# Attention and a linear-attention layer side by side: a build-time scheduler in place of a fixed slot order, seven pooled PSUM banks, unpadded projections, short first and last units

## Chip, cores and metric

The kernel runs on one core of one Trainium2 chip. The metric is the device time of one execution in microseconds, taken without the profiler; the median of three runs counts. The profile is of another execution, with the profiler on.

## What is computed

Two independent layers on 2048 tokens of width 512, with 32 heads of 16 features each, written side by side into one output of 2048 x 1024.

```python
def _A_ref(x, wqkv, wo):          # softmax attention
    qkv = (x @ wqkv).reshape(B, S, 3, H, Dh).transpose(2, 0, 3, 1, 4)
    q, k, v = qkv[0], qkv[1], qkv[2]
    scores = jnp.einsum("bhqd,bhkd->bhqk", q, k) * Dh ** -0.5
    p = softmax(scores, axis=-1)
    o = jnp.einsum("bhqk,bhkd->bhqd", p, v)
    return o.transpose(0, 2, 1, 3).reshape(B, S, D) @ wo

def _B_ref(x, wqkv, w_phi, wo):   # linear attention
    ...
    pq = jnp.einsum("bhsd,hdf->bhsf", q, w_phi)
    pk = jnp.einsum("bhsd,hdf->bhsf", k, w_phi)
    phi_q = concatenate([softmax(pq), softmax(-pq)])
    phi_k = concatenate([softmax(pk), softmax(-pk)])
    kv = jnp.einsum("bhsf,bhsd->bhfd", phi_k, v)
    z  = jnp.einsum("bhsf->bhf", phi_k)
    num = jnp.einsum("bhqf,bhfd->bhqd", phi_q, kv)
    den = jnp.einsum("bhqf,bhf->bhq", phi_q, z)[..., None] + 1e-6
    return (num / den).transpose(0, 2, 1, 3).reshape(B, S, D) @ wo
```

All inputs are bf16. Nearly all of the work is in layer A: 32 heads x 2048 queries x 2048 keys of scores and exponentials.

## The kernel before

**Units and passes.** The 32 heads are taken in 8 groups of 4 (the letter g), the queries in 4 chunks of 512 (c). A unit is one group and one chunk: 32 units, ordered by chunk, then by group (line 118). Each head of a group has 32 rows of `QT` and `KT`: 16 for its features, the others for helper rows. `WQp` and `WKp` are the projection weights padded to that layout, so that one projection job (`proj`, line 318) gives the Q or K of one group and 512 tokens.

A unit has its scores computed twice. The first time (**M1**, `emit_m1`, line 715) a matmul gives 128 queries x 512 keys of a head; two heads at once fill two of PSUM's banks 0 to 3, and VectorE takes the maximum over the keys of both with one reduce of 128x1024 (`emit_r1`, line 730). 32 such pairs make a unit. Then the **maxima chain** (`emit_mchain`, line 739) runs: a row maximum on VectorE, three short GpSimd instructions that split the negated maximum into a high and a low bf16 part, a transposing DMA, and two DMAs that put both parts into helper rows of `QT`. The second time (**M2**, `emit_m2`, line 766) the matmul gives 128 keys x 512 queries with the maximum already subtracted through the helper rows, and ScalarE writes the exponential to `pT`, a ring of 16 tiles (`emit_exp`, line 779). **PV** (`emit_pv`, line 787) multiplies by V with a column of ones, four heads side by side, into bank 7. At a unit's end `emit_xev` copies bank 7 out, the sums go through two small DMAs, a logarithm and an exponential (`emit_ln`, `emit_ex`), are spread by four DMAs (line 849), and GpSimd multiplies (`emit_mul`).

**Slots.** The order is written out by hand, in the loop over `tau` at line 916. Slot `tau` holds M1 pair `tau`, the M2 pair of slot `tau - LAG`, two exponentials, perhaps a PV of 4 matmuls, perhaps a piece of a background job, fills, and the reduce of this slot's pair. `LAG` is 43: the 32 slots of a unit and `LAGX` = 11 for the maxima chain. There are 1024 M1 slots, and 46 more until the last PV (`PVLAG` = 3). M1 waits for the reduce of two slots before. M2 takes a bank from `ring_free`, which holds banks 4, 5 and 6; a background job (`bg_step`, line 280) takes one of the same three and runs one piece a slot, as a rule four matmuls of 128x512.

**Jobs** are the projections of A, the output projections, and all matmuls of layer B (`fold_job`, `fm`, `v_job`, `kv_job`, `y_job`, `ob_job`). `fm` is a chain for 128 tokens of Q or K: projection, copy, two reduces of 128x512 on VectorE (lines 462 and 464), GpSimd and ScalarE steps, spaced over later slots by hand. A new one starts every 26 slots from slot 172.

**Fills** (`emit_fill`, line 813) are matmuls on zeros that add nothing: a slot that has fewer than two groups of PV or job work gets groups of four until it has two.

**Queues.** Every engine carries out its instructions in the order in which the plan appended them; a wait stops whatever is behind it. All transfers but a few at both ends go through SP's queue, in that order too.

**The end.** The last unit's PV comes with a second set of matmuls that give the sums spread over partitions (line 804); `emit_last` (line 879) normalises and finishes the last four output tiles.

Of the kernel before, what the change touches and what calls it, by code (L numbers as in the profile page):

```python
# [1 line left out]

# [4 lines left out]
ALU = mybir.AluOpType  # L7
# [86 lines left out]

def bass_concat_heads__softmax_full_mha__linear_kernel_hedgehog__prompt_kernel(
# [8 lines left out]
    NKT = S // 128  # L104
    NKC = S // 512
    NQC = S // 512
    NQ = 8 * NKC
    NB = 4 * NKT
    NU = NG * NQC
    RING = 16  # L110
    LAGX = 11
    PVLAG = 3
    RMLAG = 1
    NCOL = 2
    LAG = NQ + LAGX
    FM0 = 172
    FMSTEP = 26
    units = [(g, c) for c in range(NQC) for g in range(NG)]

    with contextlib.ExitStack() as es:  # L120
# [8 lines left out]
        P.add_stream("sp", None)  # L129

        def dsem(name):
            P.add_stream(name, es.enter_context(nc.semaphore("d_" + name)), 16)
            return name

        def last_tok(key):
            s = P.streams[key]
            clock = dict(s.known)
            clock[key] = s.seq
            return _Tok(key, s.seq, clock)

        PS = es.enter_context(nc.psum_tensor("PS", [128, 8, 512], F32))
        bank_reader = {}

        ones_t = sb("ones_t", [128, 128], BF)
        ident = sb("ident", [128, 128], BF)
        zmv = sb("zmv", [128, 512], BF)
        bias_k = sb("bias_k", [128, 1], F32)
        eps_t = sb("eps_t", [128, 1], F32)
# [5 lines left out]
        WQp = sb("WQp", [128, 4, NG, 128], BF)  # L154
        WKp = sb("WKp", [128, 4, NG, 128], BF)
# [9 lines left out]
        part = sb("part", [128, 2, 4, 4, NKC], F32)  # L165
        mrow = sb("mrow", [128, 2, 16], F32)
        trow = sb("trow", [128, 2, 16], F32)
        BD = sb("BD", [128, 4, 128], BF)
        woB = sb("woB", [128, 4, 512], BF)
        qmask = sb("qmask", [128, 4], F32)  # L170
        pB = sb("pB", [128, 2, 512], F32)
        uB = sb("uB", [128, 2, 1024], F32)
# [4 lines left out]
        vB = sb("vB", [128, 4, 544], BF)  # L177

        def flat(t):
# [3 lines left out]
        wqf = flat(WQp)  # L183
        wkf = flat(WKp)
# [3 lines left out]
        Wf = wkf.rearrange("p (x t c) -> p x t c", x=2, t=4)  # L188
        phiT = wqf[:, 0:2048].rearrange("p (a t s) -> p a t s", a=2, t=8)
        yB = wqf[:, 2048:3136].bitcast(F32)  # L190
        oB = wqf[:, 3136:3648]
# [6 lines left out]
        t_ones = P.op("pool", lambda e: e.memset(ones_t[:], 1.0))  # L198
        t_ident = P.op("pool", lambda e: e.affine_select(
            ident[:], ones_t[:], pattern=[[1, 128]], base=0, channel_multiplier=-1,  # L200
            compare_op=ALU.is_equal, fill=0.0), [t_ones])
        t_zmv = P.op("pool", lambda e: e.memset(zmv[:].bitcast(U32), 0))

        t_wa = {}
        wa_v = A_wqkv.rearrange("(ct p) n -> p ct n", p=128)

        def load_w(queue, i):
            t_wa[i] = P.dma(queue, dsem("wa%d" % i), lambda e: e.dma_start(
                wA[:, :, i * 512:(i + 1) * 512], wa_v[:, :, i * 512:(i + 1) * 512]))

        load_w("act", 0)
        load_w("act", 1)
        t_xa = {}
        for c in range(NQC):
            d = dsem("xa%d" % c)
            if c == 1:
                load_w("sp", 2)
            for ct in range(4):
                t_xa[c] = P.dma("sp", d, lambda e, ct=ct, c=c: e.dma_start_transpose(
                    xAT[:, ct, c * 512:(c + 1) * 512], A_x[0][c * 512:(c + 1) * 512, ct * 128:(ct + 1) * 128]))  # L220

        t_wq0 = P.op("dve", lambda e: e.memset(wqf.bitcast(U32), 0))
        t_wk0 = P.op("dve", lambda e: e.memset(wkf.bitcast(U32), 0))
        t_bias = P.op("dve", lambda e: e.tensor_reduce(
            bias_k[:, :], ident[:].rearrange("p (r x) -> p r x", x=32)[:, :, 16:18], AX.XY, ALU.add), [t_ident])

        def pad_copy(dst, col0, dep0):
            src = wA[:, :, col0:col0 + 512].rearrange("p ct (gr d) -> p ct gr d", d=16)
            dv = dst[:].rearrange("p ct g (r x) -> p ct (g r) x", x=32)[:, :, :, 0:16]
            return P.op("dve", lambda e: e.tensor_copy(dv, src), [t_wa[col0 // 512], dep0])  # L230

        t_wqp = pad_copy(WQp, 0, t_wq0)
        t_wkp = pad_copy(WKp, 512, t_wk0)

        t_stage0 = P.op("pool", lambda e: e.memset(flat(stage).bitcast(U32), 0), [t_wkp])
        t_bd0 = P.op("pool", lambda e: e.memset(flat(BD).bitcast(U32), 0))
        t_wo0 = P.op("pool", lambda e: e.memset(flat(WOp).bitcast(U32), 0))
        t_vp1 = P.op("pool", lambda e: e.memset(VP[:, :, :, 16:17], 1.0))
        t_yd1 = P.op("pool", lambda e: e.memset(Yd[:], 1.0))
        t_vb1 = P.op("pool", lambda e: e.memset(vB[:], 1.0))  # L240
        t_eps = P.op("pool", lambda e: e.memset(eps_t[:], 1e-6))
        t_qm = P.op("pool", lambda e: e.memset(qmask[:], 1.0))
        t_qm = P.op("pool", lambda e: e.affine_select(
# [9 lines left out]
        for r in range(4):  # L253
            t_wo = P.dma("sp", d_wo, lambda e, r=r: e.dma_start(
                WOp[32 * r:32 * r + 16, :, :], wo_v[r]), [t_wo0])

        calls = {}
        jobs = []  # L260
        running = []
# [741 lines left out]
```

## Time and profile before

| | us |
|---|---|
| median of three timed runs | 1343.72 |
| lowest and highest of them | 1342.71, 1344.74 |
| span of the profiled execution | 3156.6 |

The profiled execution took 2.35 times as long as the timed ones. What lies around a span (launch and end) isn't recorded. In the page, busy time is given for each engine, with its share of the span; a group of instructions has its line, its engine, output and inputs with shapes, the count, then busy time, mean ns of one, and the idle time before them with what ended it. In a timeline a row has the start, the length, engine, line and operation; rows with x2 or more are merged neighbours.

| stretch of the profiled execution, us | PE busy | DVE busy | ACT busy | granted clock |
|---|---|---|---|---|
| 0 to 30 | 28.33 | 4.84 | 1.28 | 1.00 |
| 70 to 150 | 80.00 | 16.81 | 6.43 | 1.00 |
| 300 to 600 | 300.00 | 96.61 | 97.58 | 1.00 |
| 1000 to 2000 | 999.36 | 479.75 | 461.41 | 1.00 |
| 3000 to 3156 | 155.30 | 10.07 | 57.23 | 1.00 |

The first reduce starts at 43.4 us and the last at 3013.9; the first exponential starts at 302.7 and the last at 3138.7.

### The profile page before, as it was taken

What the parts mean: (1) busy time and instruction counts of PE and PEld (TensorE: products, weight loads), DVE (VectorE), ACT (ScalarE), POOL (GpSimd) and SP (SyncE); (2) the same over time, 40 slices, a digit from 0 to 9 for tenths busy, and PEclk for the clock granted to TensorE, in tenths of its full rate; (3) what the DMA queues carried; (4) which work ended last, traced back from release to release, by engine and by line L of the source; (5) the groups of instructions that cost most, each with busy time, mean ns of one, the idle gap of its engine ahead of it and who ended that gap; (6) DMA issues with size and microseconds to landing.
All of it is one profiled execution on the core that took longest, in us unless ns stands there. A gap on an engine that the chain in (4) does not pass through costs nothing.

```text
span 3156.6 us, 29062 instructions
## 1 busy us (share of the span) xinstructions
PE 3152.2 (100%) x12226; PEld 362.2 (11%) x12226; DVE 1304.1 (41%) x1130; ACT 1296.2 (41%) x2479; POOL 307.0 (10%) x423
## 2 busy tenths in 40 slices
PE   9999999999999999999999999999999999999999
PEld 1111001111111111110011111111111111111111
DVE  1222223444444544544454435444454444445410
ACT  0001223444444444444444435444444444444442
POOL 1000000000011111111111101111111111111100
DMA  2000001000000000000000000000000000100000
GB/s 53 0 0 24 0 11 18 8 2 3 2 2 3 3 6 6 3 3 3 3 3 3 3 8 7 11 11 10 13 10 11 10 16 11 13 10 10 11 5 7
DMA packets 68939, 26.66 MB, mean 8 GB/s; under 512 B 59656, under 2 KB 66824, under 8 KB 68808
## 3 DMA queue, kind: packets, MB, share of 16 engines
q1 hardware_dynamic: 67464, 23.49, 5.4%
q8 instruction: 96, 1.57, 0.2%
q10 hardware_dynamic: 1344, 1.31, 0.1%
q14 instruction: 35, 0.29, 0.0%
HBM read 3.16 MB, written 4.19 MB: 2 GB/s over the span
## 4 chain that ended last, share of the span: by engine, by line
PE 99%; issue 0%; ACT 0%; POOL 0%; DVE 0%; POOLq 0%
PE PS L823 35%; PE PS L723 28%; PE PS L796 11%; PE PS L333 8%; PE PS L452 3%; PE PS L321 3%; PE PS L661 3%; PE PS L528 2%; PE PS L634 2%; PE PS L771 2%; PE PS L369 1%; PE PS L874 1%; PE PS L804 1%; PE PS L589 0%; PE PS L541 0%
## 5 line engine op out<-in xcount | busy, mean ns | idle before, releaser
L735 DVE TENSOR_REDUCE part<-PS 128x2 f32<-128x1024 f32 x1024 | 1255.2, 1226 | 1676.9 <-PE PS L723 1007.5
L782 ACT ACTIVATE pT<-PS 128x512 bf16<-128x512 f32 x2048 | 1111.5, 594 | 1262.1 <-PE PS L771 663.9
L823 PE MATMUL PS<-zmv,ones_t 128*17 128x512 bf16 x5004 | 1217.8, 973 | 0.3 <-ACT pT L782 0.3
L723 PE MATMUL PS<-KT,QT 32*128 32x512 bf16 x2048 | 959.5, 931 | 0.8 <-DVE QT L341 0.8
L771 PE MATMUL PS<-QT,KT 32*128 32x512 bf16 x2048 | 932.2, 902 | 0.0
L796 PE MATMUL PS<-pT,VP 128*17 128x512 bf16 x2048 | 457.2, 782 | 0.0
L723 PEld LDWEIGHTS PS<-KT,QT 32*128 32x128 bf16 x2048 | 111.0, 101 | 1580.8 <-DVE part L735 1102.9
L333 PE MATMUL PS<-xAT,WKp 128*128 128x512 bf16 x128 | 151.8, 1446 | 0.0
L823 PEld LDWEIGHTS PS<-zmv,ones_t 128*17 128x17 bf16 x5004 | 88.9, 88 | 315.1 <-issue 298.6
L771 PEld LDWEIGHTS PS<-QT,KT 32*128 32x128 bf16 x2048 | 111.1, 101 | 64.9 <-ACT pT L782 51.5
L333 PE MATMUL PS<-xAT,WQp 128*128 128x512 bf16 x128 | 116.5, 1122 | 0.0
L748 POOL TENSOR_SCALAR stage<-mrow 128x16 bf16<-128x16 f32 x32 | 8.1, 253 | 1070.4 <-DVE mrow L744 1070.4
L452 PE MATMUL PS<-WKp,xBT 128*128 128x512 bf16 x128 | 106.8, 1051 | 0.0
L345 ACT ACTIVATE KT<-PS,bias_k 128x512 bf16<-128x512 f32 x32 | 22.0, 687 | 194.9 <-PE PS L333 194.9
L507 POOL TENSOR_TENSOR wA<-eB,rB 128x1024 bf16<-128x1024 bf16 x32 | 61.7, 1929 | 398.1 <-ACT rB L501 398.1
L796 PEld LDWEIGHTS PS<-pT,VP 128*17 128x17 bf16 x2048 | 49.6, 87 | 378.0 <-issue 356.3
L321 PE MATMUL PS<-wA,xAT 128*128 128x512 bf16 x64 | 84.3, 1598 | 0.0
L859 POOL TENSOR_TENSOR QT<-X,Yd 128x256 bf16<-128x256 f32 x62 | 43.6, 725 | 400.6 <-DMA Yd<-Yd 400.4
L661 PE MATMUL PS<-WOp,QT 128*128 128x512 bf16 x96 | 80.8, 1063 | 0.0
L486 POOL TENSOR_TENSOR sB<-eB 128x512 f32<-128x512 bf16 x32 | 36.9, 1154 | 374.5 <-ACT eB L479 374.5
L471 POOL TENSOR_TENSOR uB<-pB,mB 128x512 f32<-128x512 f32 x32 | 33.9, 1058 | 395.9 <-DVE mB L462 395.9
L309 ACT ACTIVATE QT<-PS 128x512 bf16<-128x512 f32 x31 | 18.5, 597 | 93.7 <-PE PS L333 93.7
(78 smaller groups left out, 713.8 us busy)
## 6 DMA issues: line engine op xcount, KB each, us to landing
Yd<-Yd SPq DMA_DIRECT2D x124, 32.0 KB, 3.2
out_dram<-xAT SPq DMA_DIRECT2D x16, 128.0 KB, 1.7
out_dram<-OA SPq DMA_DIRECT2D x12, 128.0 KB, 1.7
wA<-in_A_wqkv_dram ACTq DMA_DIRECT2D x2, 512.0 KB, 5.0
QT<-mcols SPq DMA_DIRECT2D x64, 4.0 KB
wA<-in_A_wqkv_dram SPq DMA_DIRECT2D x1, 512.0 KB, 4.3
WOp<-in_A_wo_dram SPq DMA_DIRECT2D x4, 128.0 KB, 4.4
BD<-in_B_w_phi_dram SPq DMA_DIRECT2D x32, 0.5 KB, 1.6
```

What stands on the lines that cost most here:

```text
L321: piece = mm_piece(4, lambda e, b, ct: e.matmul(PS[:, b, :], xAT[:, ct, kt * 128:(kt + 1) * 128], wA[:, ct, 1024:1536], start=(ct == 0), s ...
L333: piece = mm_piece(4, lambda e, b, ct: e.matmul(PS[:, b, :], wpad[:, ct, g, :], xAT[:, ct, c * 512:(c + 1) * 512], start=(ct == 0), stop=( ...
L452: add_job(slot, [mm_piece(4, lambda e, b, ct: e.matmul(PS[:, b, :], xBT[:, ct, st * 128:(st + 1) * 128], Wf[:, x, ct, :], start=(ct == 0), ...
L528: piece = mm_piece(4, lambda e, b, ct: e.matmul(PS[:, b, :], xBT[:, ct, st * 128:(st + 1) * 128], wA[:, ct, 0:512], start=(ct == 0), stop= ...
L634: piece = mm_piece(4, lambda e, b, t: e.matmul(PS[:, b, :], oTB[:, i, t, :], woB[:, t, :], start=(t == 0), stop=(t == 3)), lambda: [cx["ot ...
L661: return mm_piece(4, lambda e, b, i: e.matmul(PS[:, b, :], QT[:, 4 * p + i, st * 128:(st + 1) * 128], WOp[:, 4 * p + i, :], start=(p == 0 ...
L723: tok = P.op("pe", lambda e, r=r: e.matmul(PS[:, r, :], QT[32 * r:32 * r + 32, g, q0:q0 + 128], KT[32 * r:32 * r + 32, g, kc * 512:(kc + 1 ...
L735: r1[q1] = P.op("dve", lambda e: e.tensor_reduce(part[:, u % 2, 2 * half:2 * half + 2, qt, kc], PS[:, 2 * half:2 * half + 2, :], AX.X, ALU ...
L771: m2_t[B] = P.op("pe", lambda e: e.matmul(PS[:, bank, :], KT[32 * r:32 * r + 32, g, kt * 128:(kt + 1) * 128], QT[32 * r:32 * r + 32, g, c ...
L782: exp_t[B] = P.op("act", lambda e: e.activation(pT[:, slot, :], PS[:, bank, :], ACT.Exp, scale=0.25), [m2_t[B], slot_reader.get(slot)])
L796: tok = P.op("pe", lambda e, B=B, r=r: e.matmul(PVB[32 * r:32 * r + 17, :], VP[:, kt, 4 * g + r, :], pT[:, B % RING, :], start=(kt == 0), ...
L823: P.op("pe", lambda e, cq=cq: e.matmul(PS[32 * cq:32 * cq + 17, bank, :], ones_t[:, 0:17], zmv[:, :], start=(bank != 7), stop=(bank != 7), ...
```

## The change

The loop over slots, its fixed lags and the hand-written spacing go. In their place the program, while it is being built, plays an event-driven model: every instruction is a node with an engine, what it waits for, how long it is taken to occupy its engine and when its result is taken to be there. At each event the model looks at each free engine and picks what it starts next; the order of picking becomes the order of the queues. The built kernel is still static; semaphores still guard every wait.

- **PSUM.** Bank 7 stays PV's. Banks 0 to 6 are one pool: an M1 pair wants two neighbours (or one bank at a time, then each with its own reduce of 128x512), an M2 tile one, a job one. At most 4 banks are held by M1, 3 by M2 (2 when a job is at hand), 1 by jobs.
- **TensorE's order** (`try_pe`): M1 or M2 first, by which of VectorE and ScalarE has less work waiting, then PV, the last output tile's matmuls, jobs (in pieces of two matmuls, if that doesn't delay M1), then fills, only while the array was less than 46% active over the last 3.4 us by the model's count. M2 of a unit is placed as soon as the model has its maxima landed.
- **Projections.** `WQp` and `WKp` go, with their memsets and padded copies. One job now gives eight heads (two groups) for 512 tokens, with weights straight from `wA`. Heads of even and odd number interleave in the 32-row blocks; a mask by row keeps one group's 16 rows and puts 0 or 1 in the others. For the first four groups the mask is applied as ScalarE (for the first Q, VectorE) copies out of PSUM, twice a job; for the others ScalarE copies once to `SG` and GpSimd masks twice.
- **Units.** The first and the last unit are cut into four of 128 queries: 38 units. In a short unit an M2 tile holds four key tiles x 128 queries, so that an exponential is still 128x512. The maxima of the first four may be found interleaved, as key chunks arrive.
- **Smaller ones.** The 32 loads of `w_phi` become one and four masked copies on GpSimd; the output weights of A come in eight transfers for four; layer B's scratch no longer lies in the projection weights; one `uB` buffer for two; `fm` chains are released every 31.5 us of model time from 45 us on; the end finishes one output tile for four.

```diff
-    LAG = NQ + LAGX
-    units = [(g, c) for c in range(NQC) for g in range(NG)]
+            cuts = [(0, 512)]
+            if (g, c) in ((0, 0), (NG - 1, NC - 1)):
+                cuts = [(128 * i, 128) for i in range(4)]
+            for q0, nq in cuts:
+                units.append((g, c, 512 * c + q0, nq))
...
-        t_wqp = pad_copy(WQp, 0, t_wq0)
-        t_wkp = pad_copy(WKp, 512, t_wk0)
...
-        ring_free = [4, 5, 6]
+        bank_free = {b: 0.0 for b in range(7)}
...
+        def act(out_, in_, func, cols, reads=(), writes=(), deps=(), prio=5, sbuf=False, at=0.0, **kw):
+            c = cols / 1200.0
+            return mk("act", lambda ds: P.op("act", lambda e: e.activation(out_(), in_(), func, **kw), ds),
+                      reads, writes, deps, occ=c + (0.093 if sbuf else 0.067) + (0.093 if "bias" in kw else 0.0),
+                      lat=c + (0.28 if sbuf else 0.26) + (0.093 if "bias" in kw else 0.0), prio=prio, at=at)
+
+        def dve(fn, cols, reads=(), writes=(), deps=(), prio=5, at=0.0):
+            c = cols / 960.0
+            return mk("dve", lambda ds: P.op("dve", fn, ds), reads, writes, deps, occ=c + 0.07, lat=c + 0.24,
+                      prio=prio, at=at)
...
+            j = job(quads(lambda e, b, ct: e.matmul(
+                PS[:, b, :], wA[:, ct, col:col + 128], xAT[:, ct, sl], start=(ct == 0), stop=(ct == 3))),
...
+            evac(j, act(lambda: SG[:, k, :], lambda: PS[:, j.bank, :], ACT.Copy, 512, (), [("SG", k)], prio=2))
+            for gl in range(2):
+                g = 2 * G + gl
+                if kind == "q":
+                    kq_nodes[(kind, g, c)] = pool(lambda e, g=g, gl=gl: e.tensor_scalar(
+                        T[:, g, sl], SG[:, k, :], kmask[:, gl:gl + 1], None, ALU.mult), 0.7,
+                        [("SG", k), "kmask"], [(K, g, c)], prio=1)
...
+            nf = nfree()
+            if held["m"] >= 4 or nf < 1:
+                return False
+            k = 2
+            half = sm["half"]
+            if half is not None or not pair_free() or held["m"] > 2:
+                if not single and half is None:
+                    return False
+                k = 1
...
+            dma("mt%d" % ub, lambda e: e.dma_start_transpose(mcols[:, ub, :], stage[:, ub, :]), [("stage", ub)],
+                [("mcols", ub)], prio=0, us=1.15, land=2.4)
...
+        def try_m2():
...
+            if not all(done_by(n, now) for n in mr_nodes[u]):
+                return False
+            if nfree() < 1 or held["e"] >= (EMAX - 1 if held["g"] or job_ready(now) else EMAX):
+                return False
...
+        def try_fill():
+            now = state["now"]
+            while area and area[0][0] < now - 3.4:
+                area.pop(0)
+            if "end" in state or not vz[0]:
+                return False
+            low = now < 9.0 or sum(a for _, a in area) < FILL * 3.4
...
+        def try_pe():
...
+            d, a = backlog("dve"), backlog("act")
+            TM = 3
+            TA = 3
+            for e in (("dve", "act") if d <= a else ("act", "dve")):
+                if e == "dve" and d < TM and try_m1(d < 0.3):
+                    return True
+                if e == "act" and a < TA and slots_ready() and try_m2():
+                    return True
...
+            if hurts(0.213 if pv_width() == 512 else 0.06) <= 0.03 or pv_urgent():
+                if try_pv():
+                    return True
+            if try_acc():
+                return True
+            if hurts(0.43) <= JL + job_late(now) and try_job():
+                return True
+            return hurts(0.22) <= 0.03 and try_fill()
...
-        while tau <= max(pv_in_slot) or jobs or running or calls:
-            if tau < total_q1:
-                emit_m1(tau)
...
+        while True:
+            if not events:
+                break
+            t = heapq.heappop(events)
...
+                for k in ENGS:
+                    if free[k] <= state["now"] + 1e-6:
...
+                        if try_pe() if k == "pe" else try_eng(k):
+                            go = True
```

## The prediction, made before the changed kernel was run

> **What bounds the kernel now.** I began with the page's first and fourth parts, busy times and the chain that ended last, because the profiled span is 2.3 times the median of the timed runs (1343.72 us) and that has to be understood first.
>
> ```profile
> span 3156.6 us, 29062 instructions
> PE 3152.2 (100%) x12226; PEld 362.2 (11%) x12226; DVE 1304.1 (41%) x1130; ACT 1296.2 (41%) x2479; POOL 307.0 (10%) x423
> ...
> PE 99%; issue 0%; ACT 0%; POOL 0%; DVE 0%; POOLq 0%
> ```
>
> In this execution TensorE is never idle and is the whole chain. It can't have been so in the timed runs: PE's 3152 us of work fitted into 1344. The timeline of one slot shows why.
>
> ```profile
> 908.62 1.75 PE L823 MATMUL PS<-zmv,ones_t 128*17 128x512 bf16 x8
> 908.73 1.23 DVE L735 TENSOR_REDUCE part<-PS 128x2 f32<-128x1024 f32 x1 [3.65 <-PE PS L771]
> ...
> 909.87 0.67 DVE L462 TENSOR_REDUCE mB<-pB 128x32 f32<-128x512 f32 x1
> ...
> 910.46 0.68 DVE L464 TENSOR_REDUCE mB<-pB 128x32 f32<-128x512 f32 x1
> ...
> 911.28 1.09 ACT L782 ACTIVATE pT<-PS 128x512 bf16<-128x512 f32 x2 [1.44 <-PE PS L723]
> ```
>
> Eight fills are two passes (four run side by side in the array), and later passes start about 0.84 us apart. I count passes of 512 columns from the page and the list of groups: fills 5004/4 = 1251; scores of both kinds 1067 (line 723's pair and line 771's pair run side by side); PV 512, its sums 16; full-width matmuls 726; small ones about 42. Together 3614 passes; at 0.84 us 3036 us, the rest being a slower first 300 us. Timed, a pass can have taken at most 1343.7/3614 = 0.372 us. The granted clock reads 1.00 throughout, so the record doesn't show the slowdown. [...]
>
> VectorE and ScalarE durations don't hang on that clock, so they carry the sum. The rows show what two instructions cost back to back, which is less than their durations: the reduce of 1024 starts at 908.73, the next at 909.87, so **1.14 us** (duration 1.23); the reduce of 512 costs 0.59; two exponentials together take 1.085, so a second one adds **0.49 us** (0.594 alone). Then the groups by cost:
>
> ```profile
> L735 DVE TENSOR_REDUCE part<-PS 128x2 f32<-128x1024 f32 x1024 | 1255.2, 1226 | 1676.9 <-PE PS L723 1007.5
> L782 ACT ACTIVATE pT<-PS 128x512 bf16<-128x512 f32 x2048 | 1111.5, 594 | 1262.1 <-PE PS L771 663.9
> L823 PE MATMUL PS<-zmv,ones_t 128*17 128x512 bf16 x5004 | 1217.8, 973 | 0.3 <-ACT pT L782 0.3
> ```
>
> VectorE at full pace: 1024 x 1.14 = 1167, feature-map reduces 64 x 0.59 = 38, row maxima 32 x 0.21 = 7: 1212 us, 1.18 a slot. ScalarE: 2048 x 0.49 = 1006; its other 431 instructions are 184.7 us, less some 0.10 overlap each, 142: 1148 us, 1.12 a slot. VectorE is the bound, ScalarE 5% behind.
>
> The median, split by this: about 13 us before the first reduce (the first transposed loads are issued by 5.9 us and land 2.8 later, then eight projection matmuls, one 0.69 us copy, the first scores). At the end no maxima are left for 43 slots (LAG) and three more until the last PV: 46 x 0.98 = 45 us at two exponentials a slot, then about 7 for logarithm, exponential, product, matmul, copy and output. So 1344 - 13 - 52 = 1279 us for 1024 slots, 1.249 each: VectorE idles 1279 - 1212 = **67 us** inside the slots. These three terms (13, 52, 67) are estimates; the median fixes only their sum, 132.
>
> **The change, part by part.**
>
> *Last unit in four pieces of 128 queries.* The 52 us tail becomes: the row-maximum chain of one piece, then a quarter of the exponentials. The chain now:
>
> ```profile
> 900.78 0.21 DVE L744 TENSOR_REDUCE mrow<-part 128x16 f32<-128x64 f32 x1
> ...
> 901.08 0.25 POOL L748 TENSOR_SCALAR stage<-mrow 128x16 bf16<-128x16 f32 x1 [21.38 <-DVE mrow L744]
> 901.41 0.22 POOL L750 TENSOR_TENSOR trow<-mrow,stage 128x16 f32<-128x16 f32 x1
> 901.72 0.25 POOL L751 TENSOR_SCALAR stage<-trow 128x16 bf16<-128x16 f32 x1
> 902.00 1.12 SPq L753 DMA_TRANSPOSE mcols<-stage  x1
> ...
> 904.27 1.20 SPq L756 DMA_DIRECT2D QT<-mcols  x2
> ```
>
> From 900.78 to the second DMA's issue at about 904.9; no row shows its landing. Nearest are 1.7 (output) and 3.2 us (Yd<-Yd); I take 2.0, so 6.1 + 0.1 of queueing, about 6. Then 16 exponentials x 0.49 = 8, PV and closing steps 7: **21 us**, range 20 to 23. Gain 31.
>
> *First unit in four pieces.* ScalarE's first exponential, now after 43 slots (13 + 43 x 1.249 = 67 us), comes once a 128-query piece has met all four key chunks. The last chunk's transposed loads are issued until 22.1 us and land 2.8 later, so about 26 + 6 = 33 us. But VectorE is the bound, so these 34 us only free ScalarE; I take nothing for it. Cover: VectorE's lead of 66 us over ScalarE; were that gone, the 34 us would count.
>
> The six extra units cost VectorE 6 x 0.21, ScalarE 6 x (a 128-wide copy of about 0.2, two short steps of 0.14) = 3 us, SP 6 x 8 DMA issues of 0.6 to 1.1 = some 35 us of queue, beside the other work.
>
> *Eight-head projections.* Q and K jobs drop from 64 to 32: 128 full matmuls, 128 passes off TensorE. ScalarE's copies drop from 63 to 40 (16 direct K, 2 direct Q, 22 staged): 23 x 0.49 + 16 biases x 0.09 = 13 us off. GpSimd gains 44 maskings of 128x512; the list has none. Nearest by size: 128x256 f32 at 0.725 and 128x512 at 1.06; so 32 to 47 us, I take 40. GpSimd goes from 307 to about 347 of some 1260 us: off the path unless a masking (about 1 us) stands before line 748's successors, 38 x 1 us at worst; taken at nothing, because only the order of Pool's own queue decides and the chain is put first in it. The memsets and padded copies at the head (1.76 x 2, 0.68 x 2 on VectorE) go; the first transposed load lands no earlier, and Q's first copies become two: head gain 0, range -2 to +2.
>
> *The planned order.* VectorE must still do 1024 x 1.14 + 38 + 38 x 0.21 + 1.4 = **1214 us**. A score pair may be split in two single banks: 2 x 0.59 - 1.14 = 0.04 us more each, 0 to 41 us if all were; I take 100, 4 us. What is left is the 67 us of idleness. Now M1's pair stands on PE's queue behind the M2 pair, which needs one of three banks, of which a job holds one; and a slot with a job and PV has six passes, up to 2.2 us against 1.14. There are some 240 job pieces; 67/240 = 0.28 us each. After, 32 pieces are gone, the rest come in halves of two matmuls and only when a bank is free and VectorE has work in hand. Bounds: 0 (the plan holds exactly) and 67 (it gains nothing). I take 0.08 us for each of 208, **16 us**, nearer the lower end because fills leave too: TensorE's passes fall from 3614 to about 2200 plus fills, at most 0.372 x 2200 = 818 us of 1260.
>
> Sum: 13 + 1214 + 4 + 16 + 21 = **1268 us**, 76 less than 1344 (31 tail, 51 idleness, 6 dearer on VectorE).
>
> **Rivals.**
>
> *A. Idleness stays at 67 us.* It would if it comes from signal latencies between PE and VectorE. For it: line 723's weight load waits 1102.9 us for VectorE in the list of waits, so the two hand over every slot. Against: that is a slow-pass execution. 1252 + 67 = 1319.
>
> *B. The plan holds exactly*: 1248. For it: 1.14 and 0.49 repeat to 0.01. Against: DMA landings scatter (transpose of the maxima 2.2 to 4.1 us).
>
> *C. Slower: M2 at the head of TensorE's queue.* The next unit's M2 waits for its maxima. Today LAGX gives the chain 11 slots, 13.7 us for about 6. The new order issues M2 when the chain is planned to end, without that slack; behind the waiting M2 stand M1 and PV, so VectorE starves once its two filled pairs (2.3 us) are used. 38 units x (lateness - 2.3): slower than before from (1346.4 - 1268)/38 = 2.1, a lateness of 4.4 us a unit. The transpose's worst is 1.8 over its median, which speaks against; SP's queue, where chain DMAs can stand behind a transfer waiting for ScalarE (782.5 us of such waits at line 834), speaks for. At 5.5 us late: 1268 + 38 x 3.2 = 1390.
>
> *D. TensorE becomes the bound.* With 2200 passes, a pass longer than 1214/2200 = 0.55 us would do it; at 0.60 it gives 1320 + 34 = 1354. In the trace the granted clock never falls, but the fills never stop either. [...]
>
> **How the numbers follow.** Forecast 0.58, A 0.20, B 0.08, C 0.09, D 0.05. C is all slower; of D I give 0.02 to slower, 0.01 to same, 0.02 to faster. So faster 0.88, same 0.01, slower 0.11, with 0.2% (2.7 us) as what a measurement of this kernel tells from none. The range holds forecast, A and B: from B less 4 us of pitch error, 1244, to A plus 5, 1324; it leaves out C and most of D, 0.14.
>
> **What would show it.** Right: if the profile is again of the slow kind, its span falls to passes x 0.84, (2200 + some 500 fills) x 0.84 = about 2270 us; if not, VectorE is busy 95% or more between its first and last reduce, starts the last 20 to 23 us before the end, and most of its idle time is short. A shows as short gaps before nearly every reduce; C as long gaps of VectorE and ScalarE together once a unit, ended by the maxima's DMA; D as a chain of waits on TensorE with a granted clock of 0.5. Wrong also if Pool's maskings end waits of the maxima chain, or if pairs are split far more than 100 times.

## The result, and the profile after

The changed kernel is **slower**: 1684.63 us, median of 4 runs (1672.45 to 1725.32), against 1344.23 (1342.71 to 1345.11) for the kernel before on the same chip. The ratio is 1.2511, 95% interval 1.2453 to 1.257; it leaves out the slowest run, 1725.32 us, which was in a slow state. The forecast was 1268 with a range of 1244 to 1324. What came is the state that rival D describes, TensorE as the bound at a granted clock of 0.50 (1400 to 1500 us), but far beyond its price.

First the page of the changed kernel: its span, busy times, the granted clock in slices, the chain that ended last, and the costliest groups.

```profile
span 1685.3 us, 24949 instructions
PE 1605.2 (95%) x10027; PEld 471.6 (28%) x10085; DVE 1243.9 (74%) x1129; ACT 1247.1 (74%) x2475; POOL 368.5 (22%) x502
PEclk9997995777688955588777555556668555555557
PE 66%; DVE 19%; ACT 10%; POOL 3%; issue 1%; DMA 1%; SPq 0%; ACTq 0%; DVEq 0%; POOLq 0%
L766 DVE TENSOR_REDUCE part<-PS 128x2 f32<-128x1024 f32 x1024 | 1202.2, 1219 | 315.8 <-PE PS L1048 134.0
L327 ACT ACTIVATE pT<-PS 128x512 bf16<-128x512 f32 x2048 | 1106.8, 626 | 322.5 <-PE PS L831 153.1
L1048 PE MATMUL PS<-zmv,ones_t 32*128 32x512 bf16 x2176 | 860.6, 522 | 0.3
L831 PE MATMUL PS<-QT,KT 32*128 32x512 bf16 (+1 forms) x2432 | 769.0, 456 | 13.8 <-ACT pT L327 4.7
L758 PE MATMUL PS<-KT,QT 32*128 32x512 bf16 x2048 | 613.2, 500 | 20.0 <-DVE part L766 17.9
```

Three things are to be seen. VectorE has hardly more to do than forecast (1243.9 us busy by durations) but stands idle 316 us before its score reduces. TensorE holds 66% of the chain. And the clock row falls to 5, a granted clock of 0.5, and stays there for long stretches; the mean granted clock is 0.69. The group with the most busy time on TensorE is line 1048: 2176 **fills** that use one row group, 32 of the array's 128 rows. They compute nothing, and VectorE waits for them 134 us, ScalarE 109.

Windows of the changed kernel tie the clock to the loss. The columns are the window, its length, then busy us and counts of PE, PEld, DVE, ACT and POOL, the clock, and the DMA columns.

```profile
180.00:210.00 30.00, 29.16 (x231) 10.07 (x229) 30.00 (x30) 30.00 (x65) 24.86 (x29) 1.00 0.01 2
600.00:700.00 100.00, 99.15 (x494) 25.94 (x492) 70.41 (x64) 69.94 (x139) 20.69 (x28) 0.52 0.10 14
1400.00:1500.00 100.00, 99.94 (x497) 25.95 (x491) 63.13 (x54) 66.39 (x124) 3.59 (x8) 0.50 0.06 5
```

At 1.00 VectorE and ScalarE are busy 30.00 of 30 us, as the plan meant. At 0.50 TensorE is busy 99.94 of 100 us and the other two for about two thirds of it. Over windows of 5 us between 60 and 1300 us, VectorE is busy 99% of the time in the 89 windows at full clock (1.00) and 68% in the 119 at half (0.50); the other 40 lie between.

What TensorE does at half clock (0.50), from its timeline in the changed kernel (start, length):

```profile
1400.96 0.60 PE L831 MATMUL PS<-QT,KT 32*128 32x512 bf16 x1
1401.35 1.91 PE L1048 MATMUL PS<-zmv,ones_t 32*128 32x512 bf16 x4
1403.18 0.61 PE L888 MATMUL PS<-pT,VP 128*17 128x512 bf16 x4
```

The four products of line 888 run side by side and take 0.61 us together. The four fills before them run one after another and take 1.91, each on 32 of the array's 128 rows. TensorE is "99.94 of 100 us busy" here in time, not in rows.

Where the clock is lost first, and the head, from the same timeline; the bracket is the idle time and what ended it:

```profile
1.30 0.61 PE L1203 MATMUL PS<-zmv,ones_t 128*128 128x512 bf16 x1 [1.30 <-POOL h L369]
11.75 1.86 PE L433 MATMUL PS<-xAT,wA 128*128 128x512 bf16 x4 [9.85 <-DMA xAT<-in_A_x_dram]
...
146.99 0.40 PE L522 MATMUL PS<-BD,wA 128*128 128x128 bf16 x4 [2.20 <-DMA wA<-in_B_wqkv_dram]
```

At 147 us one job waits 2.20 us for a weight load, with everything else behind it on TensorE's queue; the clock reads 0.78 in the microsecond from 148 and 0.50 from 149 to about 172. In the head only one warm-up matmul is issued (22 before the change), TensorE is idle 9.85 us, and the first four projection matmuls take 1.86 us, where four more at 19.24 us take 1.03; the record reads 1.00 for both.

At the other end, the last reduce of scores ends at 1578.6 us, 106.7 before the end of the span; this list of ScalarE's groups in that last stretch has the reason.

```profile
L327 ACT ACTIVATE pT<-PS 128x512 bf16<-128x512 f32 x117 | 64.8, 602 | 27.8 <-PE PS L831 18.2 <-PE PS L1048 9.6
```

117 exponentials of 2048 are still to come when VectorE is through.

### The profile page after: what moved, and what is told of

Read it like the earlier page. It is cut to its first block, busy times and chain, and to the rows that moved or that the text cites. A ratio compares the mean times of both kernels' runs of the same rounds, so it can differ in the third digit from the quotient of the medians.

```text
span 1685.3 us, 24949 instructions
## 1 busy us (share of the span) xinstructions
PE 1605.2 (95%) x10027; PEld 471.6 (28%) x10085; DVE 1243.9 (74%) x1129; ACT 1247.1 (74%) x2475; POOL 368.5 (22%) x502
## 4 chain that ended last, share of the span: by engine, by line
PE 66%; DVE 19%; ACT 10%; POOL 3%; issue 1%; DMA 1%; SPq 0%; ACTq 0%; DVEq 0%; POOLq 0%
PE PS L1048 22%; DVE part L766 17%; PE PS L831 17%; PE PS L758 10%; PE PS L888 10%; ACT pT L327 8%; PE PS L536 2%; POOL QT L463 2%; PE PS L645 2%; PE PS L632 1%; PE PS L433 1%; PE PS L472 1%; DVE mB L547 1%; DVE mB L549 1%; ACT KT L327 0%
## 5 line engine op out<-in xcount | busy, mean ns | idle before, releaser
L766 DVE TENSOR_REDUCE part<-PS 128x2 f32<-128x1024 f32 x1024 | 1202.2, 1219 | 315.8 <-PE PS L1048 134.0
L1048 PE MATMUL PS<-zmv,ones_t 32*128 32x512 bf16 x2176 | 860.6, 522 | 0.3
L831 PE MATMUL PS<-QT,KT 32*128 32x512 bf16 (+1 forms) x2432 | 769.0, 456 | 13.8 <-ACT pT L327 4.7
L758 PE MATMUL PS<-KT,QT 32*128 32x512 bf16 x2048 | 613.2, 500 | 20.0 <-DVE part L766 17.9
L1048 PEld LDWEIGHTS PS<-zmv,ones_t 32*128 32x128 bf16 x2176 | 223.1, 114 | 227.9 <-issue 187.2
L831 PEld LDWEIGHTS PS<-QT,KT 32*128 32x128 bf16 x2432 | 176.8, 100 | 369.6 <-ACT pT L327 236.0
L888 PE MATMUL PS<-pT,VP 128*17 128x512 bf16 (+1 forms) x2432 | 262.8, 452 | 0.4
L938 POOL TENSOR_TENSOR QT<-X,Yd 128x256 bf16<-128x256 f32 (+1 forms) x67 | 45.5, 696 | 244.9 <-ACT pT L327 88.6
L536 PE MATMUL PS<-Wf,xBT 128*128 128x512 bf16 x115 | 47.8, 525 | 4.2 <-issue 2.5
L645 PE MATMUL PS<-WOp,QT 128*128 128x512 bf16 x113 | 36.0, 443 | 2.8 <-issue 1.2
```

Source lines behind the costliest of these rows:

```text
L536: j = job(quads(lambda e, b, ct: e.matmul(PS[:, b, :], xBT[:, ct, st * 128:(st + 1) * 128], Wf[:, x, ct, :], start=(ct == 0), stop=(ct == ...
L645: j = job(quads(lambda e, b, i: e.matmul(PS[:, b, :], QT[:, i, st * 128:(st + 1) * 128], WOp[:, i, :], start=(i == 0), stop=(i == 7)), 8), ...
L758: fns = [lambda e, rr=rows[i], b=banks[i]: e.matmul(PS[:, b, :], QT[32 * rr:32 * rr + 32, g, q0 + 128 * qt:q0 + 128 * qt + 128], KT[32 * r ...
L766: d = dve(lambda e: e.tensor_reduce(part[:, ub, off + m:off + m + k], PS[:, banks[0]:banks[-1] + 1, :], AX.X, ALU.max), 512 * k, (), (), d ...
L831: fns = [lambda e, kt=kg * ns + j, j=j: e.matmul(PS[:, bank, j * nq:(j + 1) * nq], KT[32 * r:32 * r + 32, g, kt * 128:(kt + 1) * 128], QT[ ...
L888: fns.append(lambda e, r=r, s=s, kt=kt, j=j: e.matmul(PS[32 * r:32 * r + 17, VB, 0:nq], VP[:, kt, 8 * (g // 2) + 2 * r + g % 2, :], pT[:, ...
```

## The experiments

The theory after this result: **TensorE's clock follows the share of the array's rows at work, not TensorE's busy time; the new order spreads the score matmuls and makes its fills of single row groups, so the array is too empty, and once the clock is at half the work no longer fits.** The rivals: the fills' removal alone (their number), the DMA waits alone, or simply too many instructions on TensorE. Each run below is one kernel. Times are to be read beside the kernel before on the same chip, 1340 to 1352 us. Where no range is given, a measured time is that of a single run; single runs of the kernel before lie between 1334 and 1352 us here, so a difference of under some 20 us between two such times says little.

**The kernel before, profiled again.** The profile shown before the prediction had passes 0.84 us apart, so I wanted one at the pace of the timed runs; no edit.

> The kernel before, unchanged, for a profile of it at the pace of its timed runs. Clock theory (the changed kernel lost its time because the TensorE clock fell to half): here the granted clock stays at 1.00 over the whole span, a full pass takes some 0.22 us, the span is about 1342 us and VectorE is idle about 67 us between its first and last reduce. Order theory (the waits of the planned queue order cost the time, the clock only follows): the clock of the kernel before says nothing, it may fall below 1.00 here too without the time changing.

Measured: 1345.73 us. Its page:

```profile
span 1343.9 us, 29062 instructions
PE 1213.5 (90%) x12226; PEld 342.9 (26%) x12226; DVE 1225.8 (91%) x1130; ACT 1214.7 (90%) x2479; POOL 307.4 (23%) x423
PEclk9999999999999999999999999988998999889899
```

Hence a trace of before that can be compared: first reduce at 11.9 us, last one ending at 1288.9, 55 us after it. The clock isn't at 1.00 over the whole span, as I had expected, but 0.975 in the mean: 1.00 until about 785 us, with short dips later.

**Before without fills.** The 5004 matmuls on zeros of line 823 are left out.

```diff
 def emit_fill(ngroups):
+    return
```

> The kernel before without its fills (5004 matmuls on zeros less, same output). Clock theory: the fixed slot order loses the clock as well; granted clock between 0.5 and 0.7, time 1450 to 1700 us. Order theory: the slot order is as good as before, so 1320 to 1345 us, whatever the clock.

Measured: 1480.95 us, clock 0.649. So the fixed order, too, loses 140 us when its fills go, although VectorE and ScalarE do the same work; with them the clock was 0.975.

**After without fills** (after the first 9 us; matmuls on zeros only).

```diff
-low = now < 9.0 or sum(a for _, a in area) < FILL * 3.4
+low = now < 9.0
```

> The changed kernel with no fills after its first 9 us. Clock theory in its plain form: the clock is lower still (0.5 to 0.6) and the time no better than 1640 us. Clock theory with the fills as a part of the loss (at half clock 2176 one-row fills of 0.43 us stand in the queue): clock near 0.5, but 1430 to 1580 us. Order theory: the waits stay, 1650 to 1700 us.

Measured: 1510.09 us, clock 0.611. The clock is lower than with the fills (0.69), and yet the kernel is 175 us *faster*. The one-row fills thus cost more than they hold up, which is the second of the two forms of the theory; the plain form, 1640 us or more, is out.

**After with column fills at a higher limit.** The branch for one-row fills is shut, so that fills are four matmuls side by side on all 128 rows (17 columns each), and the limit under which they are placed is raised.

```diff
-if state["mode"] == "row" and pv["open"]:
+if False and state["mode"] == "row" and pv["open"]:
...
-FILL = 0.46
+FILL = 0.90
```

> The changed kernel with its one-row fills replaced by the four-column fills of the kernel before, and wherever the plan finds room (limit 0.90 of the array's activity for 0.46). Clock theory: granted clock above 0.9 and 1330 to 1400 us. Order theory: clock better, time still above 1550 us.

Measured: 1456.17 us, clock 0.819, with 767 fill passes in place of 573. That is between the two theories' ranges: the clock is lower than the clock theory had it (above 0.9, 1330 to 1400 us), the time shorter than the order theory had it. And **the same at the old limit** (only the first of the two edits), 553 passes:

> The changed kernel with its one-row fills replaced by four-column fills, at its own limit of 0.46: 553 passes for 573 by the plan's count. If one-row fills are what fails (serial at half clock, little of the array): clock 0.75 to 0.85, 1440 to 1520 us. If the amount alone decides: clock 0.69 and 1650 to 1700 us.

Measured: 1493.35 us, clock 0.753. At nearly the same number of passes the shape alone is worth 191 us (1684.6 to 1493.4), and the clock rises by 0.06.

**A probe of the clock.** It computes nothing of the two layers; the outputs are zeros. VectorE reduces 1024 elements in beats of 1.13 us, and in each beat TensorE gets a fixed load; every load stands behind ten heavy beats and again behind eight empty ones.

```diff
+for shape, k in TESTS:
+    for _ in range(10):
+        tick("h", 4)
+    for _ in range(30):
+        tick(shape, k)
+    for _ in range(8):
+        tick("f", 0)
+    for _ in range(30):
+        tick(shape, k)
```

> A probe of the clock alone: nothing of the layers is computed, the output is zeros. VectorE beats time with reduces of 1.14 us; on each beat TensorE runs k matmuls of one kind on zeros. Twelve kinds, each for 30 beats after 10 beats of four full matmuls, and again for 30 beats after 8 beats without any. Kinds: full 128x128, k 1 to 3; four 17-column ones side by side, k 1 to 3; single 32-row ones, k 2, 4, 5; four 32-row ones side by side, k 1 to 3. If the clock goes by how long TensorE is busy, four or five single 32-row matmuls a beat (75 to 95% busy) hold the full clock as well as three full ones (57%). If it goes by the part of the array that works, the 32-row ones fall to half at every k (at most 24% of the array), four rows side by side behave as full ones do, and the edge lies between one and three passes a beat. Whatever falls to half at k and rises again only at a higher k shows a lock-in.

Windows behind the heavy beats (no ScalarE columns, as it does nothing here): full matmuls, one and two a beat; four blocks of 17 columns, one and two; and single row groups, four a beat.

```profile
20.00:30.00 10.00, 4.77 (x8) 0.83 (x9) 10.00 (x10) 0.00 (x0) 0.50 0.00 0
120.00:130.00 10.00, 5.45 (x18) 1.02 (x18) 10.00 (x10) 0.00 (x0) 1.00 0.00 0
290.00:300.00 10.00, 5.48 (x36) 0.91 (x36) 10.00 (x10) 0.00 (x0) 0.50 0.00 0
380.00:390.00 10.00, 5.50 (x72) 1.00 (x72) 10.00 (x10) 0.00 (x0) 1.00 0.00 0
650.00:660.00 10.00, 10.00 (x25) 3.36 (x23) 7.32 (x6) 0.00 (x0) 0.50 0.00 0
```

The last row decides: TensorE is busy 10.00 of 10 us with single row groups, VectorE waits for it, and the clock stays at 0.50. Two full passes a beat hold 1.00 with TensorE busy 5.45 us. Three full matmuls together took 0.82 us and one alone 0.39, so passes start 0.215 us apart at full clock; in that measure one pass a beat is 0.215/1.13 = 19% of the array and read 0.50, two are 38% and read 1.00, also after the empty beats (60 to 90 and 160 to 180 us). The blocks of 17 columns, with the same two readings, count like full width. Four row groups side by side, one and two a beat, gave 0.50 and 1.00 as well.

**A finer probe**, also without the layers: two full matmuls a beat of 288 to 448 columns, and holes of one to four empty beats in a load of three passes (57%).

> Computes nothing of the layers: output is zeros. Beats of 1.13 us as in the first probe. Part one: two full 128-row matmuls per beat of 288, 320, 352, 384, 416 and 448 columns (21, 24, 26, 28, 31 and 33% of the beat at full clock), each after a heavy stretch and again after 9 us of nothing. Part two: three full matmuls per beat (57%), broken by 1, 2, 3 or 4 empty beats. Theory (a floor on the share of the array's rows at work in a window of a few us): one width from which the clock comes back, between 24 and 33%, the same after heavy and after nothing; a hole of one beat keeps the clock, one of three or four drops it. Rival (any TensorE wait of about 2 us drops it): already the holes of one and two beats drop the clock.

The windows are at 384 and 448 columns; the timeline rows are those behind a hole of one and of two beats, and the last window follows the second.

```profile
256.00:266.00 10.00, 7.25 (x19) 1.18 (x18) 10.00 (x10) 0.00 (x0) 0.50 0.00 0
410.00:420.00 10.00, 8.21 (x19) 1.18 (x18) 10.00 (x10) 0.00 (x0) 0.50 0.00 0
```

```profile
499.51 0.59 PE L129 MATMUL PS<-zmv,ones_t 128*128 128x512 bf16 x2 [1.66 <-DVE part L151]
...
557.87 0.82 PE L129 MATMUL PS<-zmv,ones_t 128*128 128x512 bf16 x3 [2.56 <-DVE part L151]
558.99 4.30 PE L129 MATMUL PS<-zmv,ones_t 128*128 128x512 bf16 x12 [0.30 <-DVE part L151]
```

```profile
559.00:562.00 3.00, 3.00 (x8) 0.98 (x9) 3.00 (x3) 0.00 (x0) 0.50 0.00 0
```

All widths fell to 0.50, 448 columns (2 x 448/512 x 0.215/1.13 = 33%) too. So the highest share that fell is **33%**, and the lowest that held, in the first probe, **38%**; I had expected the clock back between 24 and 33%. A hole of one beat left the clock at 1.00. TensorE was idle about 1.4 us there: the row shows two of that beat's three matmuls, and its 1.66 us counts the missing first one as idle time. A hole of two beats, 2.56 us, dropped the clock to 0.50 within 1 us of the work's return, for some 3.4 us; those of three and four beats, 3.69 and 4.81 us, lowered it too (0.55 from 620 to 624 us, 0.80 from 680 to 684). Each length of hole was tried once. Theory and rival both hold a part: at 33% and less the clock fell and stayed at 0.50 for as long as the load lasted (25 beats here), and at 57% a hole of 2.56 us cost a dip, as waits of 2.20 us in the changed kernel and 2.09 us in the kernel before were followed by 0.50 (149 to about 172 us; 1203 to 1209 us). In both probes all operands are constants, so what data do to the clock isn't tested.

With this measure the kernels can be placed. Every matmul of one row group, and of one block of 17 columns, is counted as a quarter pass: four side by side took 0.39 us at 1.00, as one full matmul did. The list is the changed kernel from 1400 to 1500 us.

```profile
L1048 PE MATMUL PS<-zmv,ones_t 32*128 32x512 bf16 x155 | 75.0, 623 | 0.1
L831 PE MATMUL PS<-QT,KT 32*128 32x512 bf16 x120 | 49.5, 612 | 0.0
L758 PE MATMUL PS<-KT,QT 32*128 32x512 bf16 x106 | 45.0, 617 | 0.0
L888 PE MATMUL PS<-pT,VP 128*17 128x512 bf16 x116 | 17.6, 596 | 0.0
```

497 quarters are 124 passes, x 0.215 = 26.7 us of work in 100: 27%, less than the 33% that fell in the probe, with TensorE full. With this mix of work there is no time left in which the share could rise; elsewhere in the changed kernel the clock did return, as at 172 us. The same count for 180 to 210 us, at full clock, is 44%; for the kernel before from 500 to 600 us it is 170 + 460 + 170 + 172 quarters and 24 full passes, 57%; both are above the 38% that held. My reading of the trap: at half clock the same plan does its work over more time, which lowers the share further (27% for 44%).

**After with fills owed.** Column fills placed after every second score pair ahead of other work, limit 0.90, 22 warm-up matmuls, third weight load on SP's queue: 1133 passes.

```diff
+if owed[0] >= 1 and pv["open"]:
+    owed[0] -= 1
+    pe_op([lambda e, q=q: e.matmul(
...
+    owed[0] += 0.5
```

> The changed kernel with four-column fills that are owed, one for every second score pair, and placed before M1 and M2 (1133 passes of fills in all), 22 warm-up matmuls, and the third weight load moved behind the first transposed loads as before. The plan itself is longer by it (1407 against 1314 us). Clock theory: clock above 0.93 and at most 25 us over its plan, 1400 to 1435 us; first reduce at 12 to 14 us for 18.9. Order theory: clock above 0.93, but 1500 us or more.

Measured: 1512.63 us, clock 0.851. A miss: with almost as many fills as before the change (1251) the kernel got slower than with 767, and TensorE was busy 96% of the span. So the number of fills isn't all: forced in, they push other work aside, and what is left over are second scores. From the first reduce to the end of the last one the kernel took 1310.2 us, less than the 1327.2 with 767 passes; but then 285 exponentials were left (160 there), and the tail took 185.7 us (108.8 there), at a clock of 0.57. Why there is no room for them, the score matmuls show: in the same four windows (180 to 210, 230 to 245, 480 to 520, 550 to 590 us, together 125 us) both kinds of scores occupied TensorE for 54.89 us in the kernel before and 82.81 in the changed one. The fixed order issues a pair of first scores and a pair of second scores together, four row groups side by side; the planner issues each when its own bank comes free, so they overlap in part only.

**Scores kept together.** A second-score block is placed only within 0.3 us of a first-score pair, or when ScalarE has less than 0.7 us of work ahead; column fills, limit 0.90; head as in the run before.

```diff
+    pair[0] = now + 0.3
...
-if e == "act" and a < TA and slots_ready() and try_m2():
+if e == "act" and a < TA and (a < 0.7 or now < pair[0] or m1["u"] >= NU) and slots_ready() and try_m2():
```

> The planned kernel with three edits: column fills in place of one-row fills at a limit of 0.90 (as before), 22 warm-up matmuls and the third weight load on SP (as before), and in the planner's choice a second-score block is placed only within 0.3 us after a first-score pair, or when ScalarE has under 0.7 us of work ahead: four rows then run side by side. It places 1205 fill passes; its planner ends at 1342 us. Theory (the planned order spreads the score matmuls over TensorE's time and leaves no room for fills): score matmuls take under 55% of TensorE's time at full clock instead of 66%, granted clock at 0.93 or more, time 1345 to 1385. Rival (the order is dense enough, but any waits of a greedy plan drop the clock whatever the fills): clock stays near 0.85, time 1450 or more.

```profile
span 1367.7 us, 29526 instructions
PE 1302.4 (95%) x12296; PEld 404.5 (30%) x12385; DVE 1210.8 (89%) x1129; ACT 1210.2 (88%) x2475; POOL 369.2 (27%) x502
PEclk9999698989998999899999999999999999999557
```

Measured: 1369.54 us, clock 0.933, and the scores took 69.94 of the 125 us (56%, where I had said under 55; in the last of the four windows the clock was 0.88). The theory's time was 1345 to 1385, the rival's 1450 or more. With some 1200 fill passes, about as in the run with fills owed, the time is 143 us less. Against the run at the same limit without the rule (1456.17) it is 87 us less, of which the head can be 4.1 (first reduce at 18.4 and 14.3): the order made room, in which the same limit places 1205 passes instead of 767. From some 580 us on, the clock is at 0.9 or more in every slice until VectorE is through, at 1252.7 us; after that it is lost (0.52 from 1300 to 1350 us). **With 0.6 us** in place of 0.7 (1367 passes):

> The same with 0.6 us in place of 0.7: 1367 fill passes, planner's end 1369 us. Theory: clock at 0.95 or more, time 1370 to 1400, bound by ScalarE held back by the rule. Rival (waits drop the clock): 1450 or more, no better than with 0.7.

Measured: 1412.3 us, clock 0.913. A miss, by 12 us above the range: the tighter rule holds ScalarE back more than I took. The stretch between the first and the end of the last reduce hardly changed (1243.9 us, clock 0.95, against 1238.4 and 0.96), but 230 exponentials were left behind it for 173, and the tail was 152.0 us for 115.0.

**A fourth bank for second scores.** In the run with 0.7 us, 173 exponentials were left when the last reduce ended, and 115 us followed.

```diff
-EMAX = 3
+EMAX = 4
```

> The planned kernel with paired scores and column fills (0.7 us), and ScalarE may hold four of the seven banks instead of three. Its planner ends at 1327 us (1342 without), with the last first-score reduce at 1276 instead of 1240 and 1069 reduces, so 45 pairs split. Theory (the long tail is ScalarE's backlog, which comes from waiting for second scores for want of a bank; the work only moves): last reduce near 1290, tail 50 to 65 us instead of 115, time 1340 to 1362, clock 0.92 or more. Rival (the backlog comes from TensorE's order or clock, not from banks): tail still over 100 us, or the clock falls below 0.9 and the time is 1380 or more.

```profile
span 1326.1 us, 29244 instructions
PE 1280.7 (97%) x12161; PEld 397.0 (30%) x12161; DVE 1218.1 (92%) x1174; ACT 1201.1 (91%) x2475; POOL 368.9 (28%) x502
PEclk9999989889997999999999899989998999999977
```

Measured: **1331.54 us** (1327.85 to 1339.84, 5 runs) against 1340.69, ratio 0.9931, 0.9881 to 0.998. That is 8 us under the theory's range, which had put the last reduce near 1290. The last reduce ends at 1271.2, 55 us before the end, with 74 exponentials left; 45 pairs are split. The backlog was one of banks: with three, second scores waited for a free one while VectorE's first scores held four. So the planned order with these edits is a little faster than the kernel before, by 0.7%.

**The kernel before with one number changed.** Its late dips have a cause that the repeated profile shows at TensorE:

```profile
1199.81 0.63 PE L771 MATMUL PS<-QT,KT 32*128 32x512 bf16 x2
1202.53 0.35 PE L589 MATMUL PS<-xAT,WQp 128*128 128x68 bf16 x4 [2.09 <-DMA WQp<-wA]
...
1205.70 1.04 PE L823 MATMUL PS<-zmv,ones_t 128*17 128x512 bf16 x8
```

A job stands at the head of TensorE's queue 2.09 us before its transposed feature map has landed; behind it eight fills take 1.04 us, at a clock of 0.50, where they took 0.61 before.

```diff
-add_job(tau + 5, *y_job(st, cx, hf), cols=1)
+add_job(tau + 10, *y_job(st, cx, hf), cols=1)
```

> The kernel before with one number changed: the job that reads the transposed feature map is queued 10 slots after its transpose is issued instead of 5. Theory (in the kernel before the late dips of the clock come from this job waiting some 2 us for its transpose at the head of TensorE's queue, ten times, 16 us in all, and about 6 us of half clock behind each): TensorE's waits for that transpose gone, granted clock 0.99, 1305 to 1327 us, the fastest so far. Rival (these waits lie beside VectorE's work, which has pairs in hand): 1340 or more.

```profile
span 1328.0 us, 28994 instructions
PEclk9999999999899999997999999999999999899999
```

Measured: **1325.5 us** (1323.64 to 1329.75, 5 runs) against 1340.72, ratio 0.9898, 0.9863 to 0.9933; clock 0.985. The time lies in the theory's range, and the waits for this transpose (16.2 us, ten times) are gone. How much of the 15 us is the waits and how much the clock behind them isn't separated. The two best versions weren't run side by side.

## Why the prediction was wrong, step by step

- **The failed step is "fills leave too", booked as a help.** The idleness term (16 us) rested on TensorE having fewer passes, at no more than 0.372 us each, the pace of a kernel whose fills never stop. In its place the runs show a stretch of 1559.7 us between the first and the end of the last reduce, at a clock of 0.69, where 1234 were forecast. Leaving fills out cost the clock: 140 us in the kernel before (0.649 for 0.975), and without any fills the changed one took 1510 (0.611). What the planner keeps is placed as one-row fills, which count a quarter, run one by one and make others wait: another 175 us. In the windows at full clock the term held: VectorE busy 99%.
- **Rival D had the outcome, but the wrong price.** It asked for a pass of over 0.55 us, from 2200 passes packed as in the fixed order and no fills. At 0.50 passes start 0.43 us apart: at 170.48 us four full matmuls (line 536) take 1.89 us, one 0.61, and (1.89 - 0.61)/3 = 0.43. That was enough, because the planned order doesn't pack four row groups (66% of TensorE's time for scores at full clock where the fixed order needs 44%) and adds 2176 one-row fills. Its sign, "a chain of waits on TensorE with a granted clock of 0.5", is what the page shows (66% of the chain on TensorE, 0.50 in the windows); no run had shown a clock below 1.00 by then, so the 0.5 in it was an assumption. Its chance, 0.05, was far too low: the profile of before itself had the counter-evidence that I read past, 5004 matmuls on zeros in a kernel that was otherwise tight.
- **The tail, 21 us, was mis-sized by itself.** It assumed ScalarE level with VectorE but for the last 16 exponentials. Left were 117 in the changed kernel (107 us), 173 with scores kept together (115 us) and 74 with a fourth bank (55 us). I had written that ScalarE is "5% behind" and the bound is VectorE, and priced no wait for its three banks.
- **The head, 13 us, came to 18.9.** One warm-up matmul instead of 22, since a fill is placed only when it doesn't hurt an engine that is waiting, and VectorE waits at the start; the first projections ran at 0.42 us a pass, (1.86 - 0.61)/3, with the record at 1.00, and two copies (1.54 us) precede the first reduce. With the warm-up and one weight load moved, together, it is 14.3.
- **VectorE's stretch came out near its sum, in part by luck.** With scores kept together 1238 us lie between the first and the end of the last reduce; forecast 1214 + 4 + 16 = 1234. At the measured pitch of 1.13 us the work is about 1203 us, without split pairs, so some 35 are idle: the work was forecast 15 too high and the idleness 19 too low. That run is 14.3 + 1238.4 + 115.0 = 1367.7, and of the 100 us that it lies over 1268 the tail has 94.
- **The split of the median of before** was 13, 67 and 52; the repeated profile has 11.9 to the first reduce, 55 behind the last one, and 1277 between, of which 1212 were counted as work, so 65 idle (nearer 75 with a pitch of 1.13). It held, as did the pitch of the reduce: nine in 10.26 us, of which the last is 1.22, so 1.13. VectorE's and ScalarE's durations kept at either pace of TensorE, as the prediction took them: median 1214 ns for the reduce and 597 for the exponential, against 1226 and 597 in the slow profile.
- **Masks on GpSimd, taken at nothing, did hold up the maxima once**, which the prediction had named as a sign of being wrong. The 28 masks of queries took 1.562 us each, where the plan counts with 0.7 and the prediction with about 1; all 44 together took 55 us against 40. In the changed kernel one unit's row maximum ends at 135.06 us, and its first GpSimd step stands behind ten masks:

```profile
124.37 15.41 POOL L463 TENSOR_SCALAR QT<-SG,kmask 128x512 bf16<-128x512 bf16 x10
139.75 0.26 POOL L796 TENSOR_SCALAR stage<-mrow 128x16 bf16<-128x16 f32 x1
```

  The chain that ended last runs through these masks (2% of the span) and on, over that unit's transposing DMA and the weight loads behind it on SP's queue, to the wait of 2.20 us at 147 us with which the clock is first lost. From 85 to 140 us VectorE was still busy 51.99 of 55 us. With scores kept together the same weight load is waited for, 3.60 us; with the fourth bank neither this wait nor that loss of the clock occurs (1.00 from 140 to 180 us, for 0.70 in the changed kernel). No run changed the masks alone, so their share of the time stays open.
- **Split pairs**: none where I took 100; 45 with the fourth bank, at a few hundredths of a us each, too little to be seen in the time.
- **The first unit in four pieces**: the first exponential starts at 43.6 us (63.6 in the repeated profile of before; forecast 33 and 67). As said, ScalarE's earlier start alone brought nothing that shows at the end.
- **Rivals A, B and C** didn't come; the maxima's DMA ends no large waits in the page of after.

## What to carry to other kernels

Before matmuls on zeros are cut or reshaped, count the array work that they add: quarter passes for one row group, whole passes for all rows, over the time of the stretch. In the probes the clock fell at 33% and held at 38%, and a plan that fits TensorE only at full clock can stay at half for long (TensorE busy 99.94 of 100 us at 0.50). Pack row groups side by side before adding fills, since staggered ones take the time that fills need (82.81 us of 125 for 54.89). And look for a job at the head of TensorE's queue that waits for a DMA (16.2 us in ten waits here): moving it later was worth 1% in a kernel that looked bound by another engine.

## What the runs showed of the hardware that I had not expected

TensorE busy 10.00 of 10 us can be too idle for its clock: with one of four row groups at work it stayed at 0.50. Blocks of 17 columns on all rows held it like full width (1.00 at two passes a beat). What a share of the array's full-clock work read was the same coming from a heavy load as coming from nothing: at 33% 0.50 both ways, at 38% 1.00 both ways. And the clock record isn't the whole pace: the first profile of the kernel before took 0.84 us a pass through 3156 us while the record read 1.00, and the head of the changed kernel 0.42; the second profile of the kernel before took 1343.9 us. What slowed the first stays open; no run here showed it again.
